# Sparse attention and swish MLP: batch 1's keys and queries by crossbar transposes, odd value tiles copied on GpSimd, and the value loads reordered

## The chip, the cores and the metric

The kernel runs on 1 core of one Trainium2 chip. The metric is the device time of one execution in microseconds, lower is better. A profiled execution also has a **span**, from its first to its last instruction; the execution's time is about 1.7 us longer than its span (243.04 and 241.3 in one and the same execution). Each execution also has a mean granted TensorE clock, 1.000 being full speed. On one core a run counts as slow when it is over 1.5% above the fastest of the same kernel; ratios use fast runs alone.

## The reference

```python
# q, k, v: (4, 8, 768, 64) fp32; w_in (512, 2048), w_out (2048, 512), beta (2048)
k_sum = k.reshape(B, H, nb, 32, D).max(axis=3)          # one summary key per block of 32
v_sum = v.reshape(B, H, nb, 32, D).mean(axis=3)         # one summary value per block
scores_l = scale * q @ k.T,  kept where |i - j| < 16    # a band around the diagonal
scores_s = scale * q @ k_sum.T + log(32)
x = softmax([scores_l, scores_s]) @ [v, v_sum]          # -> (3072, 512)
h = x @ w_in
out = (h * sigmoid(beta * h)) @ w_out
```

## The kernel before

The 3072 rows of `x` are worked in 8 **chunks** of 384 (two per batch). A chunk has an **h phase** (64 matmuls of `x @ w_in`, 10.4 us) and an **output phase** (48 matmuls with `w_out`). The attention of the *next* chunk is threaded between these matmuls, as "side" work with a position in the phase. So an h phase starts when the output phase before it is done and the next `xT`, the transposed attention output, is there.

Keys and queries need their 64 dimensions on the partitions. Batches 2 and 3 get that from a crossbar transpose, done by the DMA on the way (`k_bar`, `q_bar`, on the SyncE queue; `DMA_TRANSPOSE` in the traces), of tiles loaded in small rows (`krow`, `qrow`); batch 0 and, before the change, batch 1 from TensorE transposes of `knat` and `qnat`. GpSimd issues all the plain loads from memory, one after another, in the order of emission.

The loads of the start, and batch 0's odd value tiles:

```python
    for i in range(2): load_w_in(i)
    load_q_all(0, 1)
    for i in range(2, 4): load_w_in(i)
    for i in range(3): load_w_out(i)
    for t in range(TC + 1, NT, 2):
        load_v_odd0(t)                     # three 96 KB loads
    load_w_out(3)
    for i in range(npair):                 # clearing, on GpSimd
        clear_q2(i, nc.gpsimd); clear_kw(i, nc.gpsimd); clear_kT(npair + i, nc.gpsimd)
```

Side work of chunk 0 (`n` is a position between the 16 steps of the phase):

```python
for g in PAIRS:
    add(side_h, 2 * g, kw_prep, 0, g, 1)
    add(side_h, 1 + 2 * g, v_spread, 0, g, vm0[g], 0, TC, NT)   # VectorE, block means into the value tiles
add(side_h, 4, rest_mask)                                       # ends with a select on GpSimd
add(side_h, 7, q_two, 0, 0, 1, dve_copy, dve_copy)              # VectorE fills the queries of chunk 1
add(side_h, 9.5, q_two, 0, 2, 1, dve_copy, dve_copy)
...                                                             # scale_w_out x16, knat/qnat transposes of batch 1

def rest_mask():
    nc.vector.tensor_copy(out=mask[:], in_=near[:, None].to_broadcast([P, NT, QT]))
    nc.vector.memset(mask[0:W, 0], 0.0)
    select(mask[2 * 32:KR, NT - 1], W - 1, [[0, QT]], -1)
```

Value loads and the transpose of `x` in even chunks 2 and 4 (`hold` is a GpSimd copy of one element, which makes GpSimd wait for its source):

```python
def v_next(b=b):
    hold(xT[(b, 1)][0:1, 1, 0:1])       # behind the crossbar transpose of x
    load_v_even(b + 1)                  # 768 KB
    load_v_odd(b + 1)                   # 576 KB
add(side_o, 5.2, v_next)
...
add(side_o, 5.1, x_dma, b2, 0, c2)      # crossbar: half of x; the other half by TensorE at 9 and 9.1
```

and, in odd chunks, the sums of those values and their spreads in the output phase:

```python
add(side_o, at_v, vsum)                 # at_v = 2 (chunk 1: .5)
for g in PAIRS:
    add(side_o, at_v + .5 + g * .5, v_spread, b2, g, vms[b2], g, 0, NT)
```

## Time and profile before

| | before |
|---|---|
| time, median of 2 runs | 226.57 us (226.47 to 226.68) |
| profiled execution: time, span, clock | 228.44 us, 226.7 us, 0.992 |
| TensorE / ScalarE / VectorE / GpSimd busy | 94% / 67% / 53% / 30% |

The profiled execution is 1.9 us slower than the two timed ones, which turned out to matter. The next lines are the busy times by stretch of the kernel before, one stretch from the start of one h phase to the next (chunk 0's two phases apart): start and end, length, then busy time of TensorE, weight loads, VectorE, ScalarE and GpSimd with instruction counts in brackets, then the granted clock; the last two numbers, on the DMA, are not used here.

```profile
22.20:35.40 13.20, 12.48 (x114) 7.28 (x112) 10.96 (x35) 10.27 (x18) 7.21 (x24) 1.00 1.27 206
35.40:54.40 19.00, 17.33 (x183) 8.87 (x181) 11.79 (x30) 11.06 (x18) 10.45 (x13) 0.91 1.50 173
54.40:81.30 26.90, 26.07 (x268) 14.77 (x267) 18.00 (x52) 18.19 (x30) 5.35 (x8) 1.00 1.37 126
81.30:105.00 23.70, 23.70 (x192) 13.39 (x190) 11.00 (x27) 17.82 (x28) 4.77 (x6) 1.00 0.94 120
105.00:130.20 25.20, 24.35 (x219) 13.76 (x218) 16.56 (x51) 17.82 (x28) 12.25 (x15) 1.00 2.12 150
```

Chunk 0 is the first two lines (its h phase, then its output phase), chunks 1, 2 and 3 the others. In chunk 2 TensorE is busy for all of its 23.70 us, so no wait is left there to remove. Chunk 0's output phase has 1.67 us idle and a clock of 0.91. The view of everything that writes or reads `x_nat` gives the crossbar transposes of `x` one line, minimum, median and maximum:

```profile
DMA to landing us min/median/max: 2.8/2.8/3.7
```

### The profile page before, as it was taken

The numbers are of one execution on the slowest core, as the hardware profiler recorded it, in microseconds if no ns is written. First come the engines' busy times: TensorE is split into PE (matmuls) and PEld (weight loads), VectorE is DVE, ScalarE is ACT, GpSimd is POOL, SyncE is SP. The second block draws the span as 40 slices with busy tenths as digits, with TensorE's granted clock in tenths as the row PEclk, the third lists the DMA queues.
The fourth block names the chain that finished last, engine by engine and source line by source line (L and its number), as shares of the span: only waits on it lengthen the run. The fifth ranks groups of instructions, "written<-read, shape, count | busy, mean of one in ns | idle before, by whom it ended". The sixth has DMA issues, their size and how long they took to land.

```text
span 226.7 us, 4816 instructions
## 1 busy us (share of the span) xinstructions
PE 214.0 (94%) x1941; PEld 120.1 (53%) x1941; DVE 120.4 (53%) x346; ACT 152.3 (67%) x246; POOL 68.8 (30%) x105
## 2 busy tenths in 40 slices
PE   7985899979999899999999999999998999999994
PEld 2553565444565456555654566555654565556543
DVE  7767887836926941179709740489349340610000
ACT  2676879554798368955896288937984589648620
POOL 7995275096150050008825140019100000000000
PEclk9999999997999999999999999999999999999999
DMA  6999999999993299735999999148991900131012
GB/s 124 155 117 193 202 206 190 206 118 180 206 148 36 69 195 162 87 81 74 180 149 156 165 165 176 56 87 91 157 114 46 186 14 0 49 81 46 3 46 93
DMA packets 100566, 27.28 MB, mean 120 GB/s; under 512 B 89392, under 2 KB 97600, under 8 KB 100544
## 3 DMA queue, kind: packets, MB, share of 16 engines
q0 software_dynamic: 76320, 15.57, 88.1%
q1 hardware_dynamic: 24080, 11.35, 22.9%
q8 instruction: 15, 0.25, 0.5%
q10 hardware_dynamic: 144, 0.07, 0.1%
q14 instruction: 7, 0.06, 0.1%
HBM read 31.52 MB, written 6.29 MB: 167 GB/s over the span
## 4 chain that ended last, share of the span: by engine, by line
PE 68%; DMA 12%; POOL 8%; DVE 5%; issue 3%; ACT 2%; ACTq 0%; POOLq 0%
PE h_ps L476 32%; PE o_ps L494 28%; DMA qnat<-in_q_dram 6%; DMA w_in_sb<-in_moe_w_in_dram 6%; PE s_ps L339 3%; PE av_ps L365 2%; DVE v L422 2%; PE o_ps L508 2%; DVE attn L344 1%; POOL qnat L84 1%; ACT attn L341 1%; POOL v L117 1%; POOL knat L81 1%; PE px L382 1%; PE pk L234 1%
## 5 line engine op out<-in xcount | busy, mean ns | idle before, releaser
L494 PE MATMUL o_ps<-w_out_sb,h_sb 128*128 128x512 bf16 x368 | 90.1, 385 | 0.0
L476 PE MATMUL h_ps<-xT,w_in_sb 128*128 128x384 bf16 x512 | 86.0, 326 | 0.6 <-ACT h_sb L484 0.3
L484 ACT ACTIVATE h_sb<-h_ps,beta_sb 128x384 bf16<-128x384 f32 x128 | 74.1, 581 | 12.0 <-PE h_ps L476 4.1
L476 PEld LDWEIGHTS <-w_in_sb 128*128 128x128 bf16 x512 | 49.4, 98 | 34.0 <-issue 1.1
L494 PEld LDWEIGHTS <-h_sb 128*128 128x128 bf16 x368 | 33.3, 99 | 32.4 <-issue 1.4
L344 DVE TENSOR_TENSOR attn<-attn,mask 128x768 bf16<-128x768 bf16 x28 | 15.5, 558 | 49.9 <-ACT attn L341 48.8
L498 ACT COPY o_sb<-o_ps 128x512 f32<-128x512 f32 x23 | 13.5, 586 | 32.4 <-PE o_ps L494 29.1
L341 ACT ACTIVATE attn<-s_ps 128x768 bf16<-128x768 f32 x28 | 22.0, 811 | 3.7 <-PE s_ps L339 3.6
L270 DVE COPY q<-qTT 64x384 bf16<-64x384 bf16 x40 | 13.9, 346 | 10.8 <-DMA qTT<-qrow 10.1
L369 DVE TENSOR_TENSOR x_nat<-av_ps,r 128x384 bf16<-128x384 f32 x32 | 17.8, 557 | 1.1
L516 POOL COPY tick<-xT 1x1 bf16<-1x1 bf16 x4 | 0.7, 178 | 58.0 <-DMA xT<-x_nat 37.6
L95 POOL DMA_DIRECT2D krow<-in_k_dram x16 | 13.6, 867 | 13.5 <-DMA v<-in_v_dram 13.0
L246 DVE COPY kw<-kT 128x288 bf16<-128x288 bf16 x56 | 16.3, 388 | 0.0
L383 ACT COPY xT<-px 128x384 bf16<-128x384 bf16 x19 | 9.0, 479 | 10.4 <-PE px L382 10.4
L365 PEld LDWEIGHTS <-attn 128*64 128x64 bf16 x384 | 8.1, 111 | 11.1 <-DVE x_nat L369 5.0
L100 POOL DMA_DIRECT2D qrow<-in_q_dram x15 | 13.3, 901 | 0.6 <-issue 0.6
L339 PEld LDWEIGHTS <-kw 128*128 128x128 bf16 x168 | 11.1, 98 | 4.2
L365 PE MATMUL av_ps<-v,attn 128*64 128x65 bf16 x384 | 10.1, 198 | 3.2 <-DVE x_nat L369 2.3
L510 DVE COPY o_sb<-o_ps 128x384 f32<-128x384 f32 x1 | 0.6, 558 | 23.4 <-PE o_ps L508 23.4
L339 PE MATMUL s_ps<-q,kw 128*128 128x128 bf16 x168 | 12.8, 219 | 0.0
L149 ACT ACT_TABLE_LOAD x9 | 11.5, 1283 | 0.9 <-PEq L740 0.8
L422 DVE COPY v<-vm 32x1536 bf16<-32x1536 bf16 (+1 forms) x20 | 9.8, 518 | 0.6
(103 smaller groups left out, 177.9 us busy)
## 6 DMA issues: line engine op xcount, KB each, us to landing
out_dram<-o_sb SPq DMA_DIRECT2D x23, 256.0 KB, 2.7
v<-in_v_dram POOLq DMA_DIRECT2D x3, 768.0 KB, 11.0
w_in_sb<-in_moe_w_in_dram POOLq DMA_DIRECT2D x4, 512.0 KB, 12.3
w_out_sb<-in_moe_w_out_dram POOLq DMA_DIRECT2D x4, 512.0 KB, 18.1
qrow<-in_q_dram POOLq DMA_DIRECT2D x15, 128.0 KB, 11.7
krow<-in_k_dram POOLq DMA_DIRECT2D x16, 96.0 KB, 7.8
v<-in_v_dram POOLq DMA_DIRECT2D x2, 576.0 KB, 13.9
knat<-in_k_dram POOLq DMA_DIRECT2D x4, 192.0 KB, 4.5
```

Source lines behind the costliest of these rows:

```text
L95: nc.gpsimd.dma_start(out=krow[(b, g // 2)][:, g % 2, :, hh], in_=k_r2[b, :, :, 2 * g + hh])
L246: nc.vector.tensor_copy(out=kw[:, t::2, 0:KR], in_=src)
L270: nc.vector.tensor_copy(out=q2[r, :, hh].rearrange("p (m t) f -> p m t f", t=2), in_=t[r])
L339: nc.tensor.matmul(big[:, j // 3, j % 3 * P:(j % 3 + 1) * P], kw[:, j, :], q2[:, j].rearrange("p h q -> p (h q)"), start=True, stop=True)
L341: nc.scalar.activation(out=a.rearrange("p (k n) -> p k n", k=2), in_=big[:, :, 0:CT], func=ACTF.Exp, scale=scale)
L344: nc.vector.tensor_mul(out=av4, in0=av4, in1=mask[:, c * TC:(c + 1) * TC, None, :].to_broadcast([P, TC, 2, QT]))
L365: nc.tensor.matmul(ov[r, j // 2, hh], av4[:, j, hh], vr[:, hh, c * TC + j, 0:D + 1], start=True, stop=True)
L369: nc.vector.tensor_mul(out=x, in0=ov[:, :, :, 0:D], in1=r[:, :, :, None].to_broadcast([P, CC, 2, D]))
L422: nc.vector.tensor_copy(out=v_rows(b, g)[KR:P, :, t0:t1, 0:D], in_=vm[KR:P, 2 * i:2 * i + 2, None].to_broadcast([P - KR, 2, t1 - t0, D]))
L476: nc.tensor.matmul(h_ps[(i, ni)][:, 0:CT], w_in_sb[:, ki, ni * P:(ni + 1) * P], x[:, ki], start=(ki == 0), stop=(ki == k1 - 1))
L484: nc.scalar.activation(out=h_sb[i][:, ni], in_=hp[:, 0:CT], func=ACTF.Silu, scale=beta_sb[:, ni:ni + 1])
L494: nc.tensor.matmul(o_ps[ms][:], h_sb[i][:, ni, ms * P:(ms + 1) * P], w_out_sb[:, ni, :], start=(ni == 0), stop=(ni == k2 - 1))
```

## The change

The intent was to take batch 1's 96 transposes off TensorE (crossbar instead), to save three loads by copying batch 0's odd value tiles on GpSimd, and to load the even value tiles ahead of the `x` transpose so that the value sums can move into the h phase, where VectorE has time.

```diff
-    for i in range(3):
+    for i in range(4):
         load_w_out(i)
-    for t in range(TC + 1, NT, 2):
-        load_v_odd0(t)
-    load_w_out(3)
+    for i in range(npair):
+        load_k_rows(1, i)                # two loads
+        v_odd2(i)                        # GpSimd copies
+        clear_kT(npair + i, nc.gpsimd)
+    load_q_rows(1, 0)
+    load_v6(1)
     for i in range(npair):
         clear_q2(i, nc.gpsimd)
         clear_kw(i, nc.gpsimd)
-        clear_kT(npair + i, nc.gpsimd)
...
+    def v_odd2(g):
+        cp = nc.gpsimd.tensor_copy
+        vb, vr = v_bufs[0], v_rows(0, g)
+        cp(out=vr[0:64, :, TC + 1::2, 0:D], in_=vr[64:P, :, TC::2, 0:D])
+        for h in (2 * g, 2 * g + 1):
+            ...                          # two more copies
...
+        def v_even():
+            hold(qTT[(b + 1, 0)][0:1, 0, 0, 0:1])
+            load_v_even(b + 1)
+        def v_odd_next():
+            if i:
+                hold(xT[(b, 1)][0:1, 1, 0:1])
+            load_v_odd(b + 1)
...                                       # chunk 0: crossbars for batch 1, values held on qTT
-            def v1():
-                hold(w_out_sb[0:1, k2 - 1, 0:1])
-                load_v_even(1)
-                load_v_odd(1)
+            for g in PAIRS:
+                add(side_o, 2, k_bar, 1, g)
+            add(side_o, 2, q_bar, 1, 0)
+            add(side_o, 5.7, v_even)
+            add(side_o, 5.7, v_odd_next)
...                                       # even chunks 2 and 4
+                add(side_h, 2, v_even)
+                add(side_o, 5.2, v_odd_next)
...                                       # odd chunks 3 and 5
+                for g in PAIRS:
+                    add(side_h, 1 + 2 * g, keys, g)
+                    add(side_h, 5 + g, spread, g)
+                add(side_h, 4, vsum)
```

In chunk 1 the two crossbar transposes of `x` become TensorE transposes, since the crossbar is then busy with keys.

> **What bounds the kernel now.** I read the slices of the page first, then the waits, then the timelines of TensorE, GpSimd and VectorE between 20 and 82 us, and last the busy time by stage.
>
> ```profile
> PE   7985899979999899999999999999998999999994
> PEclk9999999997999999999999999999999999999999
> ```
>
> TensorE is busy nearly everywhere from slice 6 on. From 81.5 us an even chunk (h phase, then output phase) takes 10.4 + 13.3 = 23.65 us, with no TensorE idle time in the stage table; an odd chunk takes 10.4 + 14.8 = 25.2 us. What is loose lies before: slices 8 and 9 dip, and the granted clock falls there.
>
> ```profile
> PE pq L303 <- DMA qnat<-in_q_dram: 1.7, 1, 1.7
> POOL v L432 <- DMA w_in_sb<-in_moe_w_in_dram: 5.1, 2, 3.1
> ...
> 50.60:54.00 3.40, 3.40 (x14) 1.10 (x14) 2.54 (x4) 1.06 (x3) 3.40 (x5) 0.50 2.07 195
> ```
>
> The first line is TensorE waiting for batch 1's queries (48.0 to 49.6). The last is the stretch after it, at granted clock 0.50 for 3.4 us: 1.7 us lost beside the 1.7 us wait. So the change aims at some 3.4 us, plus the transposes that batch 1 costs TensorE. The second line matters for the rest: GpSimd stops before a transfer until an *older* transfer has landed. Its timeline:
>
> ```profile
> 21.26 0.80 POOL L432 DMA_DIRECT2D v<-in_v_dram  x1 [2.01 <-DMA w_in_sb<-in_moe_w_in_dram]
> 25.12 0.87 POOL L432 DMA_DIRECT2D v<-in_v_dram  x1 [3.06 <-DMA w_in_sb<-in_moe_w_in_dram]
> 26.90 0.83 POOL L432 DMA_DIRECT2D v<-in_v_dram  x1 [0.91 <-DMA qnat<-in_q_dram]
> 29.44 0.76 POOL L455 DMA_DIRECT2D w_out_sb<-in_moe_w_out_dram  x1 [1.71 <-DMA w_in_sb<-in_moe_w_in_dram]
> ...
> 36.41 0.23 POOL L163 TENSOR_SCALAR_AFFINE_SELECT mask<-mask 32x64 bf16<-32x64 bf16 x1
> 37.03 0.53 POOL L108 DMA_DIRECT2D v<-in_v_dram  x1 [0.39 <-DMA w_out_sb<-in_moe_w_out_dram]
> ```
>
> Counting the GpSimd transfers in program order, each of these waits is on the transfer issued eight before it (the 21st waits for the 13th, w_in piece 0; and so on): eight semaphores, used in turn. The select at 36.41 finishes the mask; it stands exactly where the program emits it, after everything emitted earlier. VectorE in the same stretch:
>
> ```profile
> 25.25 0.36 DVE L422 COPY v<-vm 32x768 bf16<-32x768 bf16 x1
> ...
> 28.43 0.36 DVE L422 COPY v<-vm 32x768 bf16<-32x768 bf16 x1
> 29.11 2.26 DVE L297 COPY q<-pq 64x384 bf16<-64x384 bf16 x4 [0.32 <-PE pq L289]
> 31.63 2.26 DVE L297 COPY q<-pq 64x384 bf16<-64x384 bf16 x4 [0.25 <-PE pq L289]
> 34.22 1.46 DVE L464 TENSOR_SCALAR w_out_sb<-w_out_sb,inv_beta 128x512 bf16<-128x512 bf16 x4 [0.33 <-DMA w_out_sb<-in_moe_w_out_dram]
> ...
> 38.43 1.19 DVE L344 TENSOR_TENSOR attn<-attn,mask 128x768 bf16<-128x768 bf16 x2 [0.53 <-ACT attn L341]
> ```
>
> VectorE spreads block means into batch 0's value tiles (first and fourth spread shown), then fills the second half's queries, scales w_out, and masks. TensorE's h phase ends at 35.4; its next instruction is the first scores, which need the query fills, done here by 33.9 with 1.5 us to spare.
>
> **What the Trainium skill says.** "DMA: Bandwidth & Descriptors", section Anatomy of one DMA: engines of the DMA do not wait on semaphores; the issuing sequencer does, before dispatch. The trace agrees: GpSimd sits idle 3.06 us at 25.12 with its next work behind it. "TensorE: Matmul & The Clock Gate", Part 1: an idle window of about 3.4 us halves the clock, a busy one of 3.4 us restores it. Here 1.6 us idle was enough, and the half clock lasted 3.4 us; I take the measured one. "DMA: Bandwidth & Descriptors", Specifications: rows under 512 B are below line rate. Batch 1's keys and queries now arrive in such rows. By issue time plus time to landing, the long-row knat and qnat landed 43.8 to 49.6 us, 5.8 us for 1152 KB; the small-row krow pieces of batch 2 landed about 0.62 us apart and qrow pieces 0.87, so 8 and 3 of them need 7.6 us. A loss of 1.8 us, paid back by the three 96 KB odd-value loads (0.65 us each, 1.9 us) that go. The transfers' total is even.
>
> **The change part by part.**
>
> *Removed for batch 1:* 32 query transposes (0.36 + 0.55 us of TensorE before 54.36) and 64 key transposes (0.44 us at 49.99, then 3 times 0.46 in the h phase); the stretch 54.36 to 66.82 shrinks from 12.46 to 10.4 us: **-2.06**. Also the wait and half clock, 3.4, and 1.35 of transposes before 54.36: **-4.7** if nothing replaces them.
>
> *Odd chunks:* the value sums and spreads of chunks 3 and 5 move from the output phase to the h phase. Odd output phases show 0.84 us of TensorE idle, against 0.0 in even ones, because VectorE does 1.25 us of casts and 2.1 of spreads between the masks. VectorE has 3.6 us free in that h phase (fills end 111.8, scores at 115.4), just enough. **-0.9 each, -1.8.** In chunk 1 the sums stay in the output phase, the two crossbar transposes of x become 6 TensorE transposes (+0.34) and av moves later: 14.69 becomes about 14.3, **-0.4**.
>
> *Even value loads earlier:* v goes out after the query crossbar (landed 94.3) and took 10.5 to 11 us in chunks 2 and 4, so it lands about 105, alongside the x crossbar that now lands at 102.5 and must land by 105.0. I charge **+0.3 each, +0.6**.
>
> *Odd value tiles of batch 0 on GpSimd, the step that decides.* Each pair's copies are emitted after two krow loads. Their first copy reads partitions 64 to 127 of the even tiles 6, 8, 10. The spread of that pair (25.25 to 28.43 above) writes partitions 96 to 127 of the same tiles, and is emitted later, so it must wait for the copy. The krow loads wait by the count of eight: with w_out piece 3 now the 21st, the eight krow loads wait for w_in 1 (24.8), the queries (26.6), w_in 2 (29.2), w_in 3 (31.7), w_out 0 (34.2), 1 (36.7), 2 (39.3) and 3. Piece 3 landed at 43.8 behind three odd loads; without their 1.9 us, 41.9. Issue 0.28 us later, 0.86 us of issuing, and a first copy of about 0.45 (estimate: the memset of 64x384 took 0.41): the four copies end near 28.3, 33.3, 38.4 and **43.6**. VectorE runs in order, so its fourth spread, and the query fills behind it, go from 28.4 to 43.6. Then fill 2.26: 46.2; fill 2.26: 48.5; w_out scaling 1.14.
>
> TensorE thus stands idle from 35.4 to 46.2 and again until 48.5 for the second scores. The old stretch 35.4 to 54.36 holds 18.96 - 1.7 - 1.7 - 1.35 = 14.2 us of work that remains. 46.3 + 14.2 + 1.7 (half clock after the idle) + about 2.1 (the wait for the second fill and VectorE's queue of masks, scaling and x) = **64.3** for the start of chunk 1, where it was 54.36: **+9.9**.
>
> *A second gate behind it:* the mask's select comes after all krow, qrow and clearing work: fourth pair's copies to 44.4, three qrow issues 2.7, v6 0.55, four rounds of clearing at 1.03: about 51.9. The first mask then ends 52.8. With the first gate, av is reached only at about 56, so this one is mostly hidden.
>
> *Sum:* 226.6 + 9.9 - 2.06 - 0.4 - 1.8 + 0.6 = **232.9 us**; I say 233.
>
> **The rivals.**
>
> *The intended gain.* If the spreads did not wait and the select came in time, 226.6 - 4.7 - 2.06 - 0.4 - 1.8 = 217.6, perhaps 219 with chunk 1 waiting for its crossbars. For it: the first 20 us are untouched and the tables above show the waits it removes. Against it: both waits follow from the order of emission and from semaphores that the trace shows at work. It would need one of these orders to be other than I read.
>
> *Only the select gates.* If the spread does not wait for the copy, TensorE stops at av (41.2) until 52.8, loses 11.6 + 1.7 us, and still skips the 4.7: chunk 1 at about 62.7, the end at 231.
>
> *The crossbar or value loads become the wait in chunk 1.* Queries land near 51, crossbar near 55, even values 8 to 11 us later, near 65. If chunk 1 began at 50 its value sums at 64 would wait; with chunk 1 at 64 all has long landed. This rival costs time only where the first one holds.
>
> *The transfers near x in even chunks* cost more than charged: up to 1 us each, 234.
>
> **Range and chances.** The 233 rests on w_out 3's landing (a transfer rate that held from 17 to 44 us, error under 1 us), the copies (0.5 us), how long the clock stays at half (1 to 2 us) and the later gains (1 to 2 us). I take 228.5 to 236.5. Slower by 2% means over 231.1: below the middle by 1.9 us, so 0.75. Within 2%: 0.20, mostly the select alone or smaller losses. Faster by 2% (under 222.0) needs my reading of the order to fail: 0.05.
>
> **What would show it.** Right: VectorE idle before the value spreads of batch 0, released by GpSimd, four times, the last near 43.6; TensorE idle from about 35.4 to 46, some 11 us; granted clock near 0.5 for 3 to 4 us after; the select near 52; chunk 1's h phase starting near 64 and taking 10.4; odd chunks 3 and 5 under 24.5; no wait for qnat. Wrong: spreads at 25 to 29 as before, or w_out 3 landing well before 41, or GpSimd passing the krow loads without waiting; then the first rival. An x crossbar that lands past the start of an h phase would show the last.

## The result

| | before | after |
|---|---|---|
| time, median of 2 runs | 226.57 us (226.47 to 226.68) | 244.3 us (243.04 to 245.55) |
| ratio of fast runs | | 1.0782 (95%: 1.0543 to 1.1021) |
| profiled execution: span, clock | 226.7 us, 0.992 | 241.3 us, 0.965 |
| second measurement (chip and rounds of set 2 below) | 227.05 us | 240.81 us, ratio 1.0520 (1.0451 to 1.0588) |

A ratio is the mean time of one kernel's fast runs over the mean of the other's fast runs of the same rounds, so it is not quite the ratio of the medians quoted. The changed kernel is slower, as predicted, but by 17.7 us where 6.4 were predicted, and outside the range, in the second measurement too. It also varies more: its executions lie between 237.6 and 245.6 us (two of the second measurement's four count as slow), those of before within 1.1 us of each other in any one set.

The slices of the page of the changed kernel (the span in 40 equal parts; TensorE's busy tenths in each, 9 being 90% or more, then its granted clock in tenths):

```profile
PE   6885890299799999999798999996999999999994
PEclk9999996569999999999999999999799999999999
```

Counted from 1, slices 7 and 8 are nearly empty where before they were full, and the clock sinks with them. New dips stand at slices 20 and 28, and the clock dips once more in slice 29. The waits of the changed kernel (who waited, for whom: total us, times, longest) name them:

```profile
DVE v L411 <- POOL v L422: 12.8, 4, 4.0
...
PE s_ps L328 <- DVE q L297: 10.4, 2, 8.9
...
PE h_ps L473 <- DMA xT<-x_nat: 3.6, 2, 2.0
PE px L371 <- DVE x_nat L358: 3.3, 4, 1.7
```

The first two are the predicted gate. GpSimd's timeline around its end (start, length, instruction, idle time before it and what ended it):

```profile
41.10 0.82 POOL L95 DMA_DIRECT2D krow<-in_k_dram  x1 [1.14 <-DMA w_out_sb<-in_moe_w_out_dram]
41.97 0.50 POOL L422 COPY v<-v 64x384 bf16<-64x384 bf16 x1
...
51.85 0.23 POOL L163 TENSOR_SCALAR_AFFINE_SELECT mask<-mask 32x64 bf16<-32x64 bf16 x1
...
56.42 2.25 POOL L433 DMA_DIRECT2D v<-in_v_dram  x1
58.67 1.79 POOL L441 DMA_DIRECT2D v<-in_v_dram  x1
```

VectorE's:

```profile
27.55 0.36 DVE L411 COPY v<-vm 32x768 bf16<-32x768 bf16 x1 [1.61 <-POOL v L422]
...
42.50 0.36 DVE L411 COPY v<-vm 32x768 bf16<-32x768 bf16 x1 [3.99 <-POOL v L422]
42.89 4.55 DVE L297 COPY q<-pq 64x384 bf16<-64x384 bf16 x8
...
57.71 3.12 DVE L461 TENSOR_SCALAR w_out_sb<-w_out_sb,inv_beta 128x512 bf16<-128x512 bf16 x4
```

And TensorE's:

```profile
45.21 0.82 PE L328 MATMUL s_ps<-q,kw 128*128 128x128 bf16 x6 [8.90 <-DVE q L297]
47.50 0.82 PE L328 MATMUL s_ps<-q,kw 128*128 128x128 bf16 x6 [1.47 <-DVE q L297]
...
61.59 0.34 PE L371 MATMUL px<-identity,x_nat 128*128 128x128 bf16 x3 [1.66 <-DVE x_nat L358]
```

The last `krow` load waits until 41.10 for `w_out`; only then come the fourth pair's copies, then VectorE's fourth spread (28.43 before, 42.50 now), then the query fills, then TensorE's scores. Further down, two GpSimd loads and VectorE's scalings of `w_out` fall on the same moment (56 to 61), and TensorE waits for VectorE again.

The stretches of the changed kernel that stand for those shown of before (chunk 0's two phases, chunks 1, 2, 3):

```profile
22.90:35.90 13.00, 12.28 (x113) 7.17 (x111) 4.50 (x18) 10.03 (x18) 7.11 (x15) 1.00 1.27 207
35.90:65.40 29.50, 17.19 (x134) 8.47 (x135) 22.14 (x51) 10.04 (x15) 22.48 (x41) 0.77 1.51 134
65.40:90.00 24.60, 24.34 (x223) 14.13 (x225) 14.91 (x49) 18.18 (x29) 4.25 (x6) 1.00 1.48 140
90.00:116.00 26.00, 23.70 (x190) 13.28 (x190) 10.47 (x30) 18.77 (x30) 5.75 (x7) 1.00 1.23 131
116.00:141.70 25.70, 24.33 (x215) 13.76 (x219) 17.18 (x48) 17.22 (x27) 11.91 (x15) 1.00 1.28 113
```

Chunk 0's output phase went from 19.00 to 29.50 us, and chunk 1 shrank from 26.90 to 24.60, both as the prediction has it. What it does not have is the fourth line: chunk 2 took 26.00 us with TensorE still busy for 23.70. The chain that ended last, in order of time (start, length, what), shows the `x` transposes of chunks 2 and 4 on the path:

```profile
108.99 6.99 DMA xT<-x_nat
116.03 2.77 PE h_ps L473 x16
...
160.21 7.27 DMA xT<-x_nat
167.53 4.45 PE h_ps L473 x16
```

Before, this transfer took 2.8 to 3.7 us and was off the path. Here it takes 7.0 and 7.3, and after the second one the first 16 matmuls of the h phase run at half clock (4.45 instead of 2.77 us).

Where the difference of the spans lies, against the prediction (us):

| | predicted | first profile | repeated profile |
|---|---|---|---|
| start of chunk 1 (54.4 before) | +9.9 | +11.0 | +11.9 |
| length of chunk 1 | -2.5 | -2.4 | -2.4 |
| chunks 2 to 5 | -1.2 | +5.8 | +1.7 |
| chunks 6 and 7 | 0 | +0.2 | +0.2 |
| sum | +6.3 | +14.6 | +11.5 |

The remaining 3.1 us between +14.6 and the 17.7 of the medians are the 1.9 by which the profile of before was slower than its median, and 1.3 by which the first profile of after (243.04) was faster than its own.

### The profile page after: what moved, and what is told of

Same layout as the page of the kernel before. It is cut to its first block, busy times and chain, and to the rows that moved or that the text cites. A ratio compares the mean times of both kernels' runs of the same rounds, so it can differ in the third digit from the quotient of the medians.

```text
span 241.3 us, 4652 instructions
## 1 busy us (share of the span) xinstructions
PE 212.1 (88%) x1828; PEld 119.3 (49%) x1851; DVE 119.3 (49%) x346; ACT 151.4 (63%) x244; POOL 80.4 (33%) x127
## 4 chain that ended last, share of the span: by engine, by line
PE 63%; DMA 17%; DVE 9%; POOL 5%; issue 2%; ACT 1%; ACTq 0%; POOLq 0%; SPq 0%
PE h_ps L473 28%; PE o_ps L491 27%; DMA w_out_sb<-in_moe_w_out_dram 8%; DMA xT<-x_nat 6%; PE s_ps L328 4%; DMA w_in_sb<-in_moe_w_in_dram 3%; PE av_ps L354 2%; DVE q L297 2%; DVE w_out_sb L461 2%; DVE v L411 2%; PE o_ps L505 1%; POOL v L117 1%; DVE x_nat L358 1%; POOL qnat L84 1%; POOL knat L81 1%
## 5 line engine op out<-in xcount | busy, mean ns | idle before, releaser
L473 PE MATMUL h_ps<-xT,w_in_sb 128*128 128x384 bf16 x512 | 87.7, 330 | 4.7 <-DMA xT<-x_nat 3.6
L491 PE MATMUL o_ps<-w_out_sb,h_sb 128*128 128x512 bf16 x347 | 86.3, 385 | 1.9 <-issue 1.2
L491 PEld LDWEIGHTS <-h_sb 128*128 128x128 bf16 x368 | 33.9, 99 | 33.9 <-issue 2.8
L495 ACT COPY o_sb<-o_ps 128x512 f32<-128x512 f32 x23 | 13.5, 585 | 26.5 <-PE o_ps L491 24.6
L330 ACT ACTIVATE attn<-s_ps 128x768 bf16<-128x768 f32 x28 | 22.1, 811 | 8.0 <-PE s_ps L328 7.9
L95 POOL DMA_DIRECT2D krow<-in_k_dram x24 | 19.9, 840 | 16.4 <-DMA v<-in_v_dram 7.1
L328 PE MATMUL s_ps<-q,kw 128*128 128x128 bf16 x168 | 13.8, 225 | 11.5 <-DVE q L297 10.4
L270 DVE COPY q<-qTT 64x384 bf16<-64x384 bf16 x48 | 16.8, 350 | 7.7 <-DMA qTT<-qrow 6.9
L328 PEld LDWEIGHTS <-kw 128*128 128x128 bf16 x168 | 11.5, 101 | 16.3 <-DVE q L297 11.0
L372 ACT COPY xT<-px 128x384 bf16<-128x384 bf16 x21 | 9.9, 479 | 13.4 <-PE px L371 13.4
L411 DVE COPY v<-vm 32x1536 bf16<-32x1536 bf16 (+1 forms) x20 | 11.3, 579 | 13.3 <-POOL v L422 12.8
L100 POOL DMA_DIRECT2D qrow<-in_q_dram x18 | 15.9, 894 | 0.6 <-issue 0.6
L246 DVE COPY kw<-kT 128x288 bf16<-128x288 bf16 x56 | 12.4, 267 | 0.0
L149 ACT ACT_TABLE_LOAD x9 | 11.5, 1283 | 1.0 <-PEq L728 0.8
```

The costliest lines, as they stand in the source:

```text
L95: nc.gpsimd.dma_start(out=krow[(b, g // 2)][:, g % 2, :, hh], in_=k_r2[b, :, :, 2 * g + hh])
L100: nc.gpsimd.dma_start(out=qrow[(b, c)][:, m], in_=q_r2[b, c, :, m])
L270: nc.vector.tensor_copy(out=q2[r, :, hh].rearrange("p (m t) f -> p m t f", t=2), in_=t[r])
L328: nc.tensor.matmul(big[:, j // 3, j % 3 * P:(j % 3 + 1) * P], kw[:, j, :], q2[:, j].rearrange("p h q -> p (h q)"), start=True, stop=True)
L330: nc.scalar.activation(out=a.rearrange("p (k n) -> p k n", k=2), in_=big[:, :, 0:CT], func=ACTF.Exp, scale=scale)
L411: nc.vector.tensor_copy(out=v_rows(b, g)[KR:P, :, t0:t1, 0:D], in_=vm[KR:P, 2 * i:2 * i + 2, None].to_broadcast([P - KR, 2, t1 - t0, D]))
```

## The experiments

Three sets, each on one chip with its own runs of before. All twelve runs gave correct results. Medians are over all executions, ratios over the fast ones alone; slow were the profiled executions of e1 and e5, two of `after_again`'s four and one of e6's four. Chunk lengths are read from the traces; "x lands" is the time from issue to landing of the crossbar transpose of `x` in chunks 2 and 4.

| run | median us | ratio to before (95%) | chunk 1 starts | lengths of chunks 2, 3, 4, 5 | x lands |
|---|---|---|---|---|---|
| before (profile) | 226.57 | 1 | 54.4 | 23.65 25.22 23.65 25.21 | 2.76, 3.14 |
| after (profile) | 244.3 | 1.0782 (1.0543-1.1021) | 65.4 | 26.05 25.67 25.83 25.96 | 6.99, 7.27 |
| *set 1: before* | 226.13 | | | | |
| e1_x_first | 241.44 | 1.0669 (1.0640-1.0698) | slow profile | slow profile | 2.75, 2.76 |
| e2_sums_back | 241.97 | 1.0705 (1.0640-1.0770) | 68.6 | 25.27 26.00 23.66 25.22 | 6.21, 4.48 |
| e3_x_by_pe | 239.09 | 1.0567 (1.0539-1.0594) | 67.6 | 24.59 24.27 23.99 24.27 | none |
| e4_copies_first | 235.97 | 1.0455 (1.0396-1.0514) | 61.8 | 26.43 26.64 25.21 24.28 | 7.38, 6.65 |
| *set 2: before* | 227.05 | | | | |
| after_again | 240.81 | 1.0520 (1.0451-1.0588) | 66.3 | 25.62 25.80 23.77 24.27 | 6.58, 5.22 |
| e5_hold_w_out | 238.49 | 1.0477 (1.0418-1.0537) | 64.8 | 26.58 25.50 25.29 24.28 | 7.52, 6.75 |
| e6_gates_open | 229.38 | 1.0083 (1.0010-1.0157) | 50.7 | 24.26 29.05 23.65 24.27 | 2.77, 4.96 |
| e7_before_even_early | 229.17 | 1.0116 (1.0056-1.0175) | 52.8 | 24.22 25.70 25.19 24.45 | 5.77, 6.66 |
| *set 3: before* | 226.82 | | | | |
| e8_before_copies | 226.69 | 0.9999 (0.9972-1.0026) | 52.4 | 23.65 25.30 23.65 25.22 | unchanged |
| e9_open_x_first | 226.48 | 1.0014 (0.9976-1.0053) | 51.1 | 24.26 25.44 23.65 25.22 | 2.74, 2.76 |
| e10_copies_even_pe | 225.29 | 0.9945 (0.9922-0.9968) | 51.3 | 23.99 24.84 23.99 24.31 | none |
| e11_half_early | 226.13 | 0.9977 (0.9953-1.0002) | 52.9 | 23.65 25.22 23.66 25.22 | 2.77, 3.84 |

The theory for chunk 0: the copies behind the `krow` loads hold VectorE's spreads (gate 1), with the mask's select behind it (gate 2). The theory for chunks 2 and 4: the early even-value load delays the `x` transpose. The rivals for the latter: the value sums' new place, and the crossbar queue itself.

### e1_x_first: even values behind the transpose again, sums back

```diff
-                add(side_h, 2, v_even)
-                add(side_o, 5.2, v_odd_next)
+                def v_next():
+                    hold(xT[(b, 1)][0:1, 1, 0:1])
+                    load_v_even(b + 1)
+                    load_v_odd(b + 1)
+                add(side_o, 5.2, v_next)
...
-                    add(side_h, 5 + g, spread, g)
-                add(side_h, 4, vsum)
+                    add(side_o, 2.5 + g * .5, spread, g)
+                add(side_o, 2, vsum)
```

> The changed kernel with its third part undone whole: even and odd value tiles both loaded behind the x crossbar of chunks 2 and 4, value sums of chunks 3 and 5 back in the output phase. The profile of the changed kernel has a span of 241.3 us, of which chunks 2 to 5 take 103.6 us against 97.7 before. Theory A (the even value load delays the x crossbar, and TensorE waits for x): these four chunks go back to about 97.7, the x crossbar lands about 2.8 us after its issue and TensorE never waits for it; span about 235.5, some 5.5 to 6 us under the changed kernel. Theory B (the sums in the h phase, through VectorE's order, are the loss): the same figure here, so this run gives the size of the part, and e2 and e3 tell A from B. If both are wrong (the loss comes from the first chunk's shift alone) the span stays near 241.

The transposes of `x` landed in 2.75 and 2.76 us and TensorE has no wait for `xT`. The mechanism is as expected. The total is not: 241.44 us. The profile fell in the slow state (span 259.1, clock 0.839), so the lengths of its chunks can't be compared, and where the expected gain went cannot be read from it. e2 and e3, of the same rounds, began chunk 1 at 67 to 69 instead of 65; with that start the time would fit, but for this kernel that is only argued.

### e2_sums_back: only the sums back in the output phase

The edit is the second half of e1's.

> The changed kernel with only the value sums and spreads of chunks 3 and 5 back in the output phase; the even value load stays ahead of the x crossbar. Theory A: the x crossbar still takes 6 to 7 us and TensorE still waits 1.5 to 2 us at the start of chunks 3 and 5, perhaps with the half clock behind it; the output phases get their 0.8 us of idle back, the late fills of chunk 3 go: span within 1.5 us of 241.3. Theory B: span near 236, as e1.

The transposes still landed late (6.21 and 4.48 us), and chunk 2 took 25.27 us. So the place of the sums is not what delays them. Chunk 5 went back to 25.22. Chunk 3 took 26.00, because its own `x` landed only in 5.09 us and TensorE waited 0.60 us for it; no value load was in flight then, but output stores and a query transpose were. So other traffic can delay `x` as well; in chunk 3 of e1, e3 and e9 it took 4.2 to 4.4 us. Chunk 1 began at 68.6 because chunk 0 began with a half clock, the wait behind the `w_out` scalings was 2.7 us here, and another half clock followed at 63.0; the total says nothing about the sums.

### e3_x_by_pe: x of chunks 2 and 4 transposed by TensorE

```diff
-                add(side_o, 5.2, v_odd_next)
+                add(side_o, 7.5, v_odd_next)
...
+            if c == 0 and b + 1 < B:
+                x_at, x_in = (7, 7, 9, 9.1), "sstm"
```

> The changed kernel, with the first two pairs of x of chunks 2 and 4 transposed by TensorE in place of the crossbar, the even value load still early and the sums still in the h phase (the odd load follows x, as it must). Theory A: no x crossbar, no wait for one; 0.34 us of transposes added per chunk; chunks 2 to 5 take 97.7 - 1.7 + 0.7, about 97, so the span falls some 6 to 7 us to about 235. Theory B: VectorE's chain stays, so the span stays at 240 to 242.

With the crossbar out of the way and the load as early as in the change, chunks 2 to 5 took 97.1 us instead of 103.5 (first profile of after) or 99.5 (second). Chunks 3 and 5 took 24.27 each, 0.95 less than before: the predicted gain of moving the sums (0.9 each) is real once nothing delays `x`. The total again hides a late chunk 1 (67.6, half clock at 61.8).

### e4_copies_first: the copies ahead of the krow loads

```diff
     for i in range(npair):
-        load_k_rows(1, i)
         v_odd2(i)
+    for i in range(npair):
+        load_k_rows(1, i)
         clear_kT(npair + i, nc.gpsimd)
```

> The changed kernel with the four GpSimd copies of odd value tiles emitted ahead of all krow loads instead of between them. Theory C (the spreads wait for the copies, the copies stand behind krow loads that wait for landings): VectorE's four spreads run by about 28, the query fills end by 36, TensorE goes on with the scores at about 36 without a wait. Then the mask's select, still behind all krow, qrow and clearing work, comes at about 50 to 52 and TensorE stands at the first av from about 42 to 52; chunk 1 starts at 61 to 63 instead of 65.6: span 237 to 239. If the select is no gate, chunk 1 starts near 51 and the span is about 227. If the copies' place is not the cause, the span stays at 241.

This opens gate 1: the fourth spread ran at 30.03 and the scores did not wait. TensorE's timeline of this run then has

```profile
50.83 0.55 PE L354 MATMUL av_ps<-v,attn 128*64 128x65 bf16 x12 [9.54 <-DVE attn L333]
```

and VectorE's

```profile
50.22 1.50 DVE L333 TENSOR_TENSOR attn<-attn,mask 128x768 bf16<-128x768 bf16 x3 [12.48 <-POOL mask L163]
```

The select ended at 50.2 and holds the masks, and through them TensorE, for 9.5 us. Gate 2 is there, and gate 1 had hidden it: opening gate 1 alone gave back 3.6 us of chunk 0 (65.4 to 61.8), not the 10.4 us that TensorE had waited behind it.

### after_again and e5_hold_w_out

`after_again` is the changed kernel unaltered; at 240.81 us it came out below the expected 243 to 245. e5 adds one wait, the one that the change had dropped, ahead of batch 1's value loads:

```diff
+            add(side_o, 5.7, lambda: hold(w_out_sb[0:1, k2 - 1, 0:1]))
             add(side_o, 5.7, v_even)
```

> The changed kernel itself, so that the others of this set have it from the same chip: about 243 to 245 us, its two earlier runs. Chunk 1 starting at 65 to 68 us depending on whether the half clock strikes once or twice in chunk 0.

> The changed kernel with one line more: GpSimd waits for the last scaled w_out tile before it issues batch 1's value loads, as the kernel before did. Theory D (VectorE's last four w_out scalings, 3.1 us instead of 1.14 in the changed kernel, are slowed by GpSimd's issuing of the value loads beside them, and TensorE waits for x behind them): the four scalings take about 1.15 us, the wait of 1.7 to 2.7 us before the third x transpose falls under 0.5, no half clock there, chunk 1 starts at 63 to 64: 2 to 4 us less than the changed kernel. Against it (the scalings are slow for a reason of their own, or something else holds x): they still take 3 us and the time is unchanged.

In `after_again` the four last scalings of `w_out` took 2.97 us and TensorE waited 1.50 us for `x_nat` behind them. In e5 GpSimd issues only after the scalings, and VectorE's timeline has

```profile
58.96 1.13 DVE L461 TENSOR_SCALAR w_out_sb<-w_out_sb,inv_beta 128x512 bf16<-128x512 bf16 x4
```

at 1.13 us, with the wait gone. The two ratios (1.0477 and 1.0520) have overlapping intervals, so the time alone does not show a gain, and e5's profiled execution counts as slow (240.65 us, 1.8% above e5's fastest), so its start of chunk 1, 64.8 against 66.3, is no proof. The other traces settle the cause: in the five whose last four scalings ran beside the issue of the value loads (both of after, e1, e2, e3) they took 2.77 to 4.15 us, and each of the two slow scalings ended 0.09 to 0.12 us after such an issue ended, 10 times of 10; in the seven with at most 0.15 us of such an issue beside them (before, e4, e5, e7, e8, e10, e11) they took 1.13 or 1.14 us, and in e6 and e9, beside smaller loads, 1.92 and 1.49. The repeat shows too how much the delay of `x` varies: in chunk 4 `x` landed in 5.22 us, just in time, and that chunk took 23.77.

### e6_gates_open: both gates opened

```diff
     for i in range(npair):
-        load_k_rows(1, i)
         v_odd2(i)
+    def batch1_loads(): ...            # krow, qrow, v6 and the clearing, as they were
...
             add(side_h, 4, rest_mask)
+            add(side_h, 4.5, batch1_loads)
```

> The changed kernel with the copies of odd value tiles first and all of batch 1's krow, qrow, v6 loads and the clearing behind the mask's select, so that both gates of chunk 0 are open. Theory C: TensorE runs through chunk 0 without the 11 us of idle; chunk 1 starts at 50 to 52, 4 us ahead of the kernel before. Then the rival of the prediction: chunk 1 waits for its query crossbar (landing about 56), even values (about 66) and odd ones (about 72), so chunk 1 lasts 27 to 30 us instead of 24.6; chunks 2 to 5 still lose their 5 us to the early even load. Time 229 to 233. If the select were a third-rate gate and something else held chunk 0, chunk 1 would still start after 60.

Chunk 1 began at 50.7, and on the same chip the ratio to before fell from 1.0520 to 1.0083: the two orders of emission account for most of the loss. Then the waits of TensorE have a new first line:

```profile
PE vm_ps L403 <- DMA v<-in_v_dram: 4.4, 2, 3.0
```

With chunk 1 early, its sums wait 1.4 us for batch 1's even values, the rival that the prediction held to cost time only in this case. The other 3.0 us are in chunk 3: GpSimd reached the even load of chunk 2 late, at 96.00, 0.1 us before the `x` transpose. That transpose landed in 2.77 us, and the load at 107.1, too late for sums in the h phase; a half clock followed, and chunk 3 took 29.05.

### e7_before_even_early: the early even load alone, on the kernel before

```diff
-                    def v_next(b=b):
-                        hold(xT[(b, 1)][0:1, 1, 0:1])
+                    def v_even(b=b):
+                        hold(qTT[(b + 1, 0)][0:1, 0, 0, 0:1])
                         load_v_even(b + 1)
+                    def v_odd_next(b=b):
+                        hold(xT[(b, 1)][0:1, 1, 0:1])
                         load_v_odd(b + 1)
-                    add(side_o, 5.2, v_next)
+                    add(side_h, 2, v_even)
+                    add(side_o, 5.2, v_odd_next)
...                                      # sums and spreads of chunks 3 and 5 into the h phase
```

> The kernel before with the third part of the change alone: even value load of chunks 2 and 4 ahead of the x crossbar, sums and spreads of chunks 3 and 5 in the h phase. Theory A: x crossbar 6 to 7 us from issue to landing instead of 2.8, TensorE waits 1.5 to 2 us for it at chunks 3 and 5 with perhaps a half clock behind one of them, chunks 2 to 5 together 102 to 104 us instead of 97.7: time 230 to 233. If the loss of these chunks came from chunk 0's shift, the time would be 225 to 226, the gain that the prediction put at 1.2 us.

Without batch 1's crossbars or copies, the `x` transposes again take 5.77 and 6.66 us, TensorE waits for them (1.8 us in two waits), and the kernel is 1.2% slower than before, under the 2% that would be called slower. Chunks 2 to 5 took 99.6 us against 97.7, so the mechanism is as expected but the loss is smaller (102 to 104 and 230 to 233 us were expected). The wait for `x` in this run, and the line of the transposes in its `x_nat` view:

```profile
PE h_ps L476 <- DMA xT<-x_nat: 1.8, 2, 1.4
DMA to landing us min/median/max: 2.8/3.3/6.7
```

So the delay needs nothing but the early load. Across all traces one pattern shows. Wherever a full even-value load had been issued 4 to 7 us ahead of an `x` transpose, the transpose landed from 0.2 us before to 0.9 us after that load, 13 times of 13:

| run, chunk | load issued, landed | x issued, landed |
|---|---|---|
| after, 2 | 103.33, 115.58 | 108.99, 115.98 |
| after, 4 | 155.86, 167.62 | 160.21, 167.48 |
| after_again, 4 | 154.57, 165.21 | 160.81, 166.03 |
| e7, 2 | 92.83, 103.16 | 98.25, 104.02 |
| e6, 2 (load only 0.1 us ahead) | 96.00, 107.11 | 96.11, 98.88 |

In the last row the load's packets had not begun to move, and `x` took 2.77 us. The times of the single packets (in the packed traces; no view of `prof` shows them) tell how. Undisturbed, the first of the transpose's 768 packets moves 1.2 us after its issue. In the 13 cases it moved 2.0 to 4.3 us after, when 89 to 98% of the load's 6144 packets had moved. In the first row that was at 112.47, with 91% moved; at 110.2, when it would have begun undisturbed, 54% had. So the transpose did not share with the load here, it came almost after it. Why the engines do so is not shown.

### e8_before_copies: the copies alone, on the kernel before

```diff
-    for i in range(3):
+    for i in range(4):
         load_w_out(i)
-    for t in range(TC + 1, NT, 2):
-        load_v_odd0(t)
-    load_w_out(3)
+    for i in range(npair):
+        v_odd2(i)
```

> The kernel before with one idea of the change alone, placed so that nothing waits for it: the three odd-value loads of batch 0 replaced by the GpSimd copies, emitted behind the fourth w_out load and ahead of the clearing. Theory C (only the copies' place among the waiting krow loads made them costly): spreads run by 30, fills end by 35 to 36, the select by 35. The w_out pieces and batch 1's keys and queries land 1.9 us earlier than 49.6, near 47 to 47.7, so TensorE's 1.7 us wait for qnat and the half clock behind it vanish: 2.5 to 3.5 us under the kernel before, 223 to 224. Rival: the copies themselves cost (they slow VectorE, or delay GpSimd) and the time stays at 226 to 228.

The queries landed at 47.5, two microseconds earlier, and the wait for them is gone. The mean did not move (ratio 0.9999). The profiled execution had a half clock at 22.1 us, at the start of chunk 0, which that of before did not; the granted clocks of the six timed runs were 0.983 to 0.992 in five, and 1.000 in one, and that one took 225.56 us, where the three runs of before at 1.000 took 226.26 to 227.03. Some 1 us of gain is thus likely at full clock, from a single run; it is not shown.

### e9_open_x_first: gates open, scalings undisturbed, values behind x

This is e6, e5 and e1 together.

> The changed kernel with all its found costs undone: copies first and batch 1's loads behind the select (as e6), the value loads of batch 1 held behind the scaled w_out (as e5), values of later batches behind the x crossbar with the sums in the output phase (as e1). What is left of the change is the crossbar for batch 1's keys and queries. Chunk 1 should start at 50.7 as in e6 and last about 26.5 (waiting for even values), chunks 2 to 5 should be 97.7 with x crossbars of 2.8 us: 222 to 224.5. If the early even load was not the cause of the loss in chunks 2 to 5, they stay at 100 to 103 and the time is 226 to 229.

At 226.48 us this equals before (1.0014) and misses the 222 to 224.5 expected. Chunk 1 began at 51.1, but took 27.08 us, not 24.6: TensorE waited there for the even values of batch 1.

```profile
PE vm_ps L403 <- DMA v<-in_v_dram: 2.2, 1, 2.2
```

Chunks 2 to 5 took 98.6. So the change has no gain left once its losses are removed but its sums stay where they were: what the crossbars save in chunk 1 is spent waiting for values.

### e10_copies_even_pe: what worked, on the kernel before

This is e8 (copies ahead of everything, no crossbars for batch 1), e7 (early even load, sums in the h phase) and e3 (`x` of chunks 2 and 4 by TensorE) together.

> A version meant to beat both: e8 with the even value load early and the sums in the h phase, and x of chunks 2 and 4 by TensorE so that no crossbar meets the load. From e3, chunks 2 to 5 take 97.1 against 97.7, so 0.5 us under e8: 222.5 to 223.5. If the early load hurts in another way than through the x crossbar (VectorE slowed by the issuing, a wait of the sums for the even values), it is above e8 by 1 to 3 us.

It is the only version whose interval lies below 1: 225.29 us, 0.9945 (0.9922 to 0.9968), over five rounds. By the 2% measure that is still the same time as before, and it misses the 222.5 to 223.5 expected. The gain is not one of clock alone: its four executions at 0.998 or more took 224.94 to 225.38 us, the four of before 226.26 to 227.03. Which of its three parts gives it is not separated. The slices of its page have no dip after the start, in TensorE or its clock:

```profile
PE   7885899999999899999999999999999999999994
...
PEclk9999999999999999999999999999999999999999
```

### e11_half_early: half of the even values early, on the kernel before

```diff
+                    def v_early(b=b):
+                        hold(qTT[(b + 1, 0)][0:1, 0, 0, 0:1])
+                        load_v_half(b + 1, 0)
...
-                        load_v_even(b + 1)
+                        load_v_half(b + 1, 1)
...
+                    add(side_h, 2, v_early)
```

> The kernel before with only half of the even value load (pairs 0 and 1) ahead of the x crossbar and the other half with the odd tiles behind it; sums in the output phase as before. If the crossbar is late because it has to share with what is still outstanding of the load (theory A), half a load, started 3 us after its issue, is mostly through by then: x takes 2.8 to 4.5 us from issue to landing in chunks 2 and 4, TensorE does not wait for it, time 226 to 227.5. If any such load in flight costs the crossbar a fixed 3 to 4 us (theory A2), it takes 5 to 7 us, TensorE waits 1 to 2 us at chunks 3 and 5, time 228 to 230.

The half loads landed at 100.34 and 150.50, the transposes at 101.11 and 151.13. They took 2.77 and 3.84 us and nobody waited (ratio 0.9977). When the first packet of the transpose moved, all of the half load's packets had moved in chunk 2, and 92% in chunk 4. A fixed penalty for any load in flight is thereby out; what is left of the load when `x` is issued fits the delays.

This run has the same wait for `qnat` in chunk 0 as before (1.61 us) but no half clock after it, and began chunk 1 at 52.9 instead of 54.4. Most timed runs of before look like it: in the three sets 16 of 25 have a clock of 0.998 or more.

### A reading across the traces: which idle windows halve the clock

The records of the clock show that half-clock stretches last 3.41 us or 3 or 4 times that, and start on a grid of 3.41 us whose phase differs between executions (the first full clock comes at 4.5 to 7.3 us). Cutting each trace into these windows and summing TensorE's idle time in each, gives this for the windows entered at full clock, in the thirteen traces other than e1's (some matmul records are missing from the traces, so a single idle time can be some tenths too high):

| idle in a window of 3.41 us | followed by half clock |
|---|---|
| 0.8 to 1.42 us | never |
| 1.43 to 1.94 us | sometimes: 1.67 (before), 1.94 (e3) yes; 1.66 (after), 1.77 (e11), 1.94 (e3, at its end) no |
| 2.01 us and more | always |

Two waits of nearly equal length can thus cost 1.7 us more or nothing: the 1.67 us of before was followed by a half clock, the 1.61 us of e11 was not, though both lay in one window. What decides between 1.43 and 1.94 us is not shown. In this range lies the start of the kernel: chunk 0 begins with a half clock in 6 of 13 traces (21.5 to 23.2 us), after windows with 1.43 to 1.81 us idle, and without one in the others, after at most 1.21 to 1.63. By an estimate from e8 and e10, which are alike until there and start chunk 1 at 52.4 and 51.3, it costs 1.2 us. e2 and e3 lost another one at 62 to 63, after 2.34 and 1.94 us.

## Why the prediction was wrong

The direction and the mechanism that decides (gate 1) were right; the size was not. By its steps:

- **"Odd value tiles of batch 0 on GpSimd, the step that decides": right.** The four spreads began at 27.55, 32.30, 37.36 and 42.50, each released by GpSimd, against "28.3, 33.3, 38.4 and 43.6". They run 0.7 to 1.1 us earlier because the loads that they hang on landed that much earlier (`w_out` piece 3 at 40.81, 41.9 said). The scores began at 45.21 and 47.50 (46.2 and 48.5 said). e6 confirms it: with the order changed, the whole delay is gone.
- **"A second gate behind it … mostly hidden": right.** The select ran at 51.85 (about 51.9 said); e4 shows what it costs when it is not hidden.
- **From the second scores to chunk 1: 17.9 us, not 15.8.** Most of this +2.1 is a term that the sum lacked. The change replaced the hold on the last scaled `w_out` by a hold on `qTT`, so GpSimd issued two value loads (4.0 us) while VectorE scaled `w_out`; the scalings took 3.12 us instead of 1.13 (e5), and TensorE waited 1.66 us. The Trainium skill has the likely cause: in "SBUF — State Buffer", section "SBUF: two separate sides", a pair of ports is shared by GpSimd and VectorE's two-port operations under an exclusive lock that one side holds for its whole instruction while the other blocks. The trace agrees: 3.12 beside the loads and 1.13 without, with the slow scalings released 0.09 to 0.12 us after the end of an issue in all five traces that have them. The half clock was mis-sized too: after the idle time it was to last "3 to 4 us" and cost 1.7; it lasted from 45.21 to 52.27, with TensorE busy for 5.37 us of it, which by an estimate cost half of that, 2.7. So the prediction's "about 2.1" for the queues was on the large side; no run separates these.
- **"Removed for batch 1: -2.06" and "-0.4" in chunk 1: right.** 24.6 us measured, 10.4 + 14.3 = 24.7 said.
- **"I charge +0.3 each, +0.6" for the early even load: this is the step that failed.** It put the load's landing at "about 105", the moment when `x` is needed, but left the transpose at its old 2.76 us. In fact the load took 10.3 to 12.8 us from issue, and `x` landed when the load landed, not 2.76 us after its own issue. In the first profile the load landed 25.6 us after chunk 2 began, in a chunk of 23.65, so `x` was 2.4 us late: in its place stands +2.4 and +2.2 for chunks 2 and 4, and, since VectorE's sums now stand in front of the fills, late fills in chunk 3 and a half clock in chunk 5. That is +5.8 in the place of -1.2. In the repeated profile the delay was +2.0 and +0.1, and these four chunks lost 1.7; e7, with the early load alone, lost 1.8. The rival "up to 1 us each, 234" named the right thing and was too small as well. The Trainium skill has a sentence that should have warned: "DMA: Bandwidth & Descriptors", section "Queues, rings and completion order", says that each DMA engine takes turns between the queues with work, a packet at a time. By that the two had to be expected to meet. But the runs show no turns: the transpose's first packet moved when 89 to 98% of the load's had. The measurement decides; why is open.
- **"-0.9 each, -1.8" for the sums of chunks 3 and 5: right where `x` is on time** (24.27 in e3 against 25.22), lost in the first profile of the changed kernel (25.67 and 25.96); in the repeated one chunk 5 took 24.27.
- **The base.** The profile of before shows a half clock in chunk 0. The three later sets have spans of before from 224.2 to 225.8 us, clock 0.99 to 1.000, and e11 shows such an execution. The 1.7 us of half clock that the change was to remove were mostly not there (16 of 25 executions of before have a clock of 0.998 or more), and the loss counts from 1.9 us lower.
- **The intended gain,** the first rival, is answered by e9: with both gates open and `x` undisturbed it came to 226.5 us, no gain, not 217.6 to 219 (of which 1.8 us, the sums' move, is not in e9). The third rival (values as the wait in chunk 1) is the reason: 1.4 us in e6, 2.2 in e9.

- **The sums.** Two are off by a little: the terms of the total give 232.84, not 232.9, and those of "only the select gates" 63.0, not 62.7 (e4, which tests it, began chunk 1 at 61.8). Nothing rests on this.

Still open: why the transpose's packets come after the load's, what decides the half clock between 1.43 and 1.94 us of idle time, and whether e8's microsecond is real.

## What to carry to other kernels

An engine that issues loads in program order is a gate: before an operation is put behind such an issue, ask what its issue waits for, and what in other engines' order stands behind that operation; keep what others wait for ahead of the loads, not after. A transfer on the path should not be issued while a large load is in flight: plan with the landing of that load, not with the transfer's own time. And before pricing a stall, look at several executions: a wait of 1.6 to 1.7 us cost 1.7 us more in one execution and nothing in another.

## What the Trainium skill lacked or had wrong

- "TensorE: Matmul & The Clock Gate", Part 1, says that a window of about 3.4 us is free-running, which agrees (a grid of 3.41 us, its phase different in each execution), and that after an idle window the clock is half. It gives no size for a partly idle window: with 2.01 us or more of idle time in 3.41 the clock was halved every time, with 1.42 or less never, between them sometimes.
- "DMA: Bandwidth & Descriptors", "Queues, rings and completion order", has queues taking turns, which these traces do not show. A crossbar transpose of 2.76 us, issued 4 to 7 us behind a 768 KB load of small rows, took 4.5 to 7.5 us; its first packet moved when 89 to 98% of the load's had, and it landed from 0.2 us before to 0.9 us after that load, in 13 of 13 cases.
- "SBUF — State Buffer", "SBUF: two separate sides", says that whichever side starts first blocks the other, but its worked example for loads is VectorE keeping GpSimd from issuing. It has no number for a GpSimd load that blocks VectorE: here four scalings took 2.77 to 4.15 us beside the issue of two value loads, and 1.13 without.
- No page says that GpSimd's loads wait for the load eight before them in programs built as this one is. It set gate 1: idle times of 1.84, 1.76, 1.39, 1.70 and 1.14 us before `krow` loads, each ended by an older load.
